# An FNet and GLU kernel: other times and rooms for the tests of its DFT matrices

## The chip, the cores and the metric

The kernel runs on one core of a Trainium2 chip. The metric is the device time of one launch in microseconds, the median of several runs. On the core PE multiplies matrices, DVE and ACT work on vectors, POOL and SP mostly issue transfers here, which 16 DMA engines carry out.

## What is computed

Two layers, each a Fourier mixing step and a gated linear unit, on x of 2048 rows by 640 columns:

```python
def _A_ref(x, dft_seq_re, dft_seq_im, dft_hid_re, dft_hid_im):
    a = jnp.einsum("bsd,ed->bse", x, dft_hid_re)
    b = jnp.einsum("bsd,ed->bse", x, dft_hid_im)
    return jnp.einsum("ts,bse->bte", dft_seq_re, a) - jnp.einsum("ts,bse->bte", dft_seq_im, b)

def _B_ref(x, w_gate, w_up, w_down):
    g = jnp.einsum("bsd,df->bsf", x, w_gate)
    u = jnp.einsum("bsd,df->bsf", x, w_up)
    return jnp.einsum("bsf,fd->bsd", _sigmoid(g) * u, w_down)

x = A_x
for _ in range(2):
    x = x + _A_ref(_layernorm(x, axis=-1), A_dft_seq_re, A_dft_seq_im, A_dft_hid_re, A_dft_hid_im)
    x = x + _B_ref(_layernorm(x, axis=-1), B_w_gate, B_w_up, B_w_down)
```

The matrices are inputs: the sequence matrices are 2048 x 2048, the hidden ones 640 x 640, the weights 640 x 1728 and 1728 x 640.

## The kernel before, in words

The kernel does not multiply by the full DFT matrices. It uses their symmetries (a row and its mirror differ by sign at most) and multiplies folded halves. Since the matrices are inputs, it also tests at run time that the symmetries hold, over the whole of them: it loads a piece and its mirror images, subtracts or adds them on DVE, and sums the squares of what is left on ACT. If at the end the sums are not small, a branch runs `general`, a plain version; with these inputs it does not run.

**The tests.** A test has three parts. `load_rows` (four transfers of 128 KB) and `load_cols` load a piece of the sequence matrices from POOL's queue, `load_hidden_rows` from POOL's and `load_hidden_cols` from SP's a piece of the hidden ones. `test_rows` (L1602, L1603, two of L1605), `test_cols` and the others compare on DVE and put what is left into the list `rest`. `square_rest` takes the oldest entries of `rest` and gives each to `square_sum` (L1579), one ACT instruction over 128 x 768 in most cases, followed by a read of its accumulator. A piece lies in a room, eight units of 128 columns of the buffer `big`. There are two rooms behind the units that the slots use, and test k uses room k % 2, so that a load waits until the square of the test before the last has run.

**The order.** `folded` is run once per layer while the program is built. It fills a list `steps` (what PE does, in order) and a table of jobs: `at(u, f, ...)` puts a job at a due time u, counted in steps. Each step then emits the jobs that are due. A gated step covers two hidden columns (`seven`) and emits its jobs in four portions. Every engine runs its instructions in the order in which they are emitted, and waits for semaphores at the head of its queue. So a due time decides behind what an instruction stands on its engine. A layer has four blocks of 512 rows, each with 14 gated steps (in layer 2 some 11.8 us for two) and 8 steps of `down` (5.6 us each); `block[b]` is the first step of block b.

**Around the tests.** In a gated step PE makes chains of matmuls in PSUM (`products`, L1389). ACT copies an unfinished chain to `big` (`snap`, L1393, 128 x 256) and PE goes on adding to the same bank when the copy is done. DVE adds parts (`part_three`, L1425 and L1426, which frees a bank), ACT takes the sigmoid (L1435), DVE multiplies (`up`, L1445 and L1447), and ACT and DVE split the result into two halves of 16 bits (L1456, L1457). The operands of the next block are made during `down` of the block before: DVE scales rows (`pair_apply`, L598), ACT and DVE split them (`pair_parts`, L616 and L617), and SP transposes them by DMA (`pair_transpose`, L623), in two rounds. Rows of the result leave by an indirect store from POOL's queue (L437). SP loads the weights of the next steps (`load_s`, L1306 to L1312).

**The slots.** All else in `big` comes from `Slots.take` and `give`. The program is built twice: a dry run records at which tick of a clock each slot is taken and given back, `find_homes` then places them, the largest product of size and time first, and prefers a home whose neighbours in time are some ticks away.

The due times of the tests, before:

```python
if first:
    free = (block[1] + 6, block[3] + 13, 42), (d0 - 0.4, d0 + 4.6, 9)
else:
    free = (block[0] + 6, block[0] + 13, 8), (block[1] + 3, block[1] + 14, 10), (block[2] - 6, block[2] + 14, 15)
```

Each triple is a stretch of steps and the number of tests in it; the stretch over the number is the pace.

Of the kernel before, what the change touches and what calls it, by code (L numbers as in the profile page):

```python
# [10 lines left out]
F16 = mybir.dt.float16  # L11
# [5 lines left out]
P = 128  # L17
# [56 lines left out]
WDU = (NF + 1) * 5  # L74
FIX = XU + 2 * XTU + WDU
NEAR = (8, 1)


class Slots:
# [5 lines left out]

    def take(self, n, high):
        k = len(self.asked)
        self.clock += 1
        self.asked.append([n, self.clock, None])
        a = self.homes[k] if self.homes else FIX  # L90
        return Slot(self.big[:, a * UNIT : (a + n) * UNIT], k)

    def give(self, s):
        self.clock += 1
        self.asked[s.k][2] = self.clock


def find_homes(asked):

    area = [n * (t1 - t0) for n, t0, t1 in asked]  # L100
    for near in NEAR:
        first = {}
        for turn in range(40):
            order = sorted(range(len(asked)), key=lambda k: (-first.get(k, 0), -area[k]))
            homes, k = place_in_order(asked, order, near)
            if k is None:
                return homes
            first[k] = first.get(k, 0) + 1
    assert False, f"no room for {asked[k]}"


def place_in_order(asked, order, near):
    homes = [None] * len(asked)
    placed = []
    for k in order:
        n, t0, t1 = asked[k]
# [109 lines left out]
def folded(ctx, tc, pool, dram, big, acc, flag, homes, x, ct, wh, wg, wu, wc, wd, out):  # L226
# [43 lines left out]
            nc.vector.scalar_tensor_tensor(dl, src, s, dh, op0=OP.mult, op1=OP.subtract)  # L270

    def start():
        nc.gpsimd.memset(room(0, 1), 0.0)
# [96 lines left out]

    def junk(n):

        v = room(0, 1).bitcast(F16)
        for _ in range(n):
            nc.tensor.matmul(acc[banks[0]][:, :256], v[:, :P], v, start=True, stop=True)

# [1202 lines left out]
        nc.scalar.activation(v, v, AF.Square, accum_out=new_sum()[:p])  # L1579

    rest = []

    def square_rest(n=1):
        for _ in range(n):
            square_sum(rest.pop(0))

    def room(k, n=CK):
        u = UNITS + CK * (k % 2)
        return big[:, u * UNIT : (u + n) * UNIT]

    def load_rows(r, k):

        v = room(k).rearrange("p (g n c) -> p g n c", g=4, n=2)
        s = 1 + 16 * k
        for g, (row, d) in enumerate(((s, 1), (S - s, -1), (HS - s, -1), (HS + s, 1))):
            nc.gpsimd.dma_start(v[:, g], bass.AP(ct.tensor, (r * S + row) * S, [[P, NS], [d * S, 16], [1, P]]))  # L1596

    def test_rows(r, k):
        v = room(k)
# [3 lines left out]
        nc.vector.tensor_tensor(d, c, d, op=same)  # L1603
        for odd in range(2):
            nc.vector.tensor_tensor(c[:, odd::2], a[:, odd::2], c[:, odd::2], op=other if odd else same)  # L1605
        rest.append(v[:, 2 * P :])

    def load_cols(r, i, k):

        n, row = (P, START[i]) if i < NB else (1, SB)  # L1610
        v = room(k).rearrange("p (g c) -> p g c", g=4)[:n]
        for g, t in ((0, 1 + 256 * k), (2, HS - 256 * (k + 1))):
            nc.gpsimd.dma_start(v[:, g : g + 2], bass.AP(ct.tensor, (r * S + row) * S + t, [[2 * S, n], [HS, 2], [1, 256]]))  # L1613

    def test_cols(r, i, k):
        v = room(k)[: P if i < NB else 1]
# [6 lines left out]
        rest.append(v[:, 256:])  # L1623

    def load_edges(r):

# [24 lines left out]

    def load_hidden_rows(r, k):

        v = room(k)[: 20 * ND].rearrange("p (g n c) -> p g n c", g=2, c=P)
        for g, (row, d) in enumerate(((1 + 80 * k, 1), (D - 1 - 80 * k, -1))):
            nc.gpsimd.dma_start(v[:, g], bass.AP(wh.tensor, (r * D + row) * D, [[P, ND], [d * D, 80], [1, P]]))

    def test_hidden_rows(r, k):
        a, b = (room(k)[: 20 * ND, 4 * P * g : 4 * P * (g + 1)] for g in range(2))
        nc.vector.tensor_tensor(b, a, b, op=OP.subtract if r == 0 else OP.add)  # L1660
        rest.append(b)

    def turns():

# [6 lines left out]

    def load_hidden_cols(r, j):
        n = P if j < 2 else EC - 2 * P
        nc.sync.dma_start(room(3 * r + j)[:n, :D], wh[r, j * P : j * P + n, :])

    def test_hidden_cols(r, j):
        a = room(3 * r + j)[: P if j < 2 else EC - 2 * P, :D]
        b = room(3 * r + j)[: P if j < 2 else EC - 2 * P, D : D + EW - 1]
        nc.vector.scalar_tensor_tensor(b, a[:, : EW - 1], turns()[: b.shape[0]], a[:, EH : EW - 1 : -1], op0=OP.mult,
                                       op1=OP.subtract if r == 0 else OP.add)  # L1680
        rest.append(b)
        nc.vector.tensor_reduce(new_max()[: a.shape[0]], a, axis=AX.X, op=OP.max, apply_absolute_value=True)  # L1682
        nc.vector.tensor_tensor(a[:, 1:EH], a[:, 1:EH], a[:, D - 1 : EH : -1], op=OP.subtract if r == 0 else OP.add)
        rest.append(a[:, 1:EH] if r == 0 else a[:, :EC])
        if r == 1 and j == 0:
            rest.append(a[0:1, EC:])
        if r == 1 and j == 2:
            drop("turns")

# [95 lines left out]
    for layer in range(2):  # L1785
# [158 lines left out]
        if first:  # L1944
            free = (block[1] + 6, block[3] + 13, 42), (d0 - 0.4, d0 + 4.6, 9)
        else:
            free = (block[0] + 6, block[0] + 13, 8), (block[1] + 3, block[1] + 14, 10), (block[2] - 6, block[2] + 14, 15)
        tests = [[(load_rows, test_rows, (r, k)) for k in range(2 * NS)] +
                 [(load_cols, test_cols, (r, i, k)) for i in range(NB + 1) for k in range(2)] for r in range(2)]
        tests = tests[0] + tests[1][:9] if first else tests[1][9:]  # L1950
        for u0, u1, n in free:
            pace = (u1 - u0) / n
            for u in [u0 + pace * k for k in range(n)]:
                load, test, key = tests.pop(0)
                at(u, load, *key)
# [188 lines left out]
```

## Time and profile before

| | before |
|---|---|
| runs, us | 1140.57, 1142.03, 1142.58 (median 1142.03) |
| profiled execution, its own time | 1143.76 us |
| its span in the trace | 1141.9 us |
| granted clock of PE | 0.996 |
| PE busy | 1110.8 us, 97% |
| DVE, ACT, POOL busy | 67%, 47%, 30% |
| bytes moved | 214.72 MB, 188 GB/s on average |

The profile is that of one execution. "Idle before" is how long an engine stood at the head of its queue before an instruction, and the arrow names what ended the wait. The DMA share is the mean busy share of the 16 DMA engines. Line numbers are those of the kernel before; in the changed kernel L598 to L1561 have moved by one.

### The profile page before, as it was taken

To read this page: it belongs to the slowest core of one execution; us is meant where nothing else is said; L and a number is where in the kernel's file an instruction comes from. 1 tells how busy PE (TensorE), PEld (TensorE's weight loads), DVE (VectorE), ACT (ScalarE), POOL (GpSimd) and SP (SyncE) were. 2 spreads that over 40 slices of the span, in tenths; PEclk is the share of its full clock that TensorE was granted. 3 is DMA by queue.
4 is the path that set the end of the run, shared out by engine and by line. 5 is a ranking of instruction groups with operands and counts; after the bars stand their busy time and mean duration, and the time that the engine had idled before them with its cause. 6 is when DMAs were issued, how large, how long until landed. Compare 5 with 4: busy or idle time off the path is not lost. (4 is left out here: it accounts for less than half of the span.)

```text
span 1141.9 us, 23440 instructions
## 1 busy us (share of the span) xinstructions
PE 1110.8 (97%) x9030; PEld 882.3 (77%) x9030; DVE 761.8 (67%) x1678; ACT 537.2 (47%) x1187; POOL 348.1 (30%) x568
## 2 busy tenths in 40 slices
PE   5889999999999999999999999999999999999998
PEld 3668446788878887788878888778877888788875
DVE  7994998856756775486667878834664568526750
ACT  6975583355524653256525545315541455225430
POOL 1001664332546452432350216021453113141000
PEclk9899999999999999999999999999999999999999
DMA  8444685967495767968621665475767864499401
GB/s 250 152 124 151 240 319 157 270 210 244 154 244 182 246 185 152 246 223 291 201 98 57 177 223 160 130 216 179 241 167 174 257 230 150 85 254 284 143 18 38
DMA packets 154447, 214.72 MB, mean 188 GB/s; under 512 B 74655, under 2 KB 99505, under 8 KB 154326
## 3 DMA queue, kind: packets, MB, share of 16 engines
q1 hardware_dynamic: 135622, 165.04, 48.4%
q0 software_dynamic: 18560, 47.93, 14.3%
q8 instruction: 72, 1.18, 0.4%
q14 instruction: 49, 0.40, 0.1%
q10 hardware_dynamic: 144, 0.16, 0.0%
HBM read 173.04 MB, written 25.44 MB: 174 GB/s over the span
## 5 line engine op out<-in xcount | busy, mean ns | idle before, releaser
L1389 PE MATMUL acc<-big 128*128 128x256 f16 x4698 | 517.1, 273 | 4.7 <-ACT big L1393 4.5
L1389 PEld LDWEIGHTS <-big 128*128 128x128 f16 x4698 | 459.6, 98 | 60.1 <-issue 5.7
L1546 PE MATMUL acc<-big 128*128 128x320 f16 x2624 | 357.7, 299 | 0.0
L1546 PEld LDWEIGHTS <-big 128*128 128x128 f16 x2624 | 256.8, 98 | 99.5
L1596 POOL DMA_DIRECT2D big<-in_ct x256 | 174.5, 687 | 270.6 <-DVE big L1605 181.3
L1393 ACT ACTIVATE big<-acc 128x256 f32<-128x256 f32 x348 | 127.7, 380 | 214.7 <-PE acc L1389 212.4
L1579 ACT ACTIVATE big<-big 128x768 f32<-128x768 f32 (+10 forms) x110 | 81.6, 742 | 113.0 <-DVE big L1605 85.5
L1457 DVE TENSOR_TENSOR big<-big 128x512 f16<-128x512 f32 x87 | 59.9, 689 | 105.9 <-ACT big L1456 105.7
L1342 PE MATMUL acc<-big 128*128 128x256 f16 (+1 forms) x705 | 114.6, 325 | 0.5 <-ACT big L672 0.5
L1342 PEld LDWEIGHTS <-big 128*128 128x128 f16 x705 | 68.9, 98 | 45.0 <-issue 0.7
L1435 ACT ACTIVATE big<-big 128x512 f32<-128x512 f32 x87 | 53.3, 627 | 49.1 <-DVE big L1426 48.2
L270 DVE SCALAR_TENSOR_TENSOR big<-big 128x640 f16<-128x640 f32 (+7 forms) x82 | 62.7, 797 | 6.7 <-ACT big L268 6.6
L1561 DVE SCALAR_TENSOR_TENSOR big<-acc,big 128x320 f32<-128x320 f32 x64 | 28.4, 483 | 57.8 <-PE acc L1546 57.8
L1445 DVE SCALAR_TENSOR_TENSOR big<-acc,big 128x256 f32<-128x256 f32 x87 | 36.3, 418 | 41.7 <-PE acc L1389 36.3
L1426 DVE TENSOR_TENSOR big<-big,acc 128x512 f32<-128x512 f32 x87 | 59.2, 681 | 2.0 <-PE acc L1389 1.8
L268 ACT ACTIVATE big<-big 128x640 f16<-128x640 f32 (+7 forms) x82 | 50.9, 657 | 17.3 <-POOL big L1283 6.5
L616 ACT ACTIVATE big<-big 128x384 f16<-128x384 f32 (+2 forms) x48 | 28.8, 648 | 64.1 <-DVE big L598 45.0
L1456 ACT ACTIVATE big<-big 128x512 f16<-128x512 f32 x87 | 54.5, 626 | 9.3 <-DVE big L1447 7.3
L1613 POOL DMA_DIRECT2D big<-in_ct x40 | 27.3, 685 | 96.9 <-ACT big L1393 73.7
L1602 DVE TENSOR_TENSOR big<-big 128x256 f32<-128x256 f32 x64 | 26.7, 416 | 27.4 <-DMA big<-in_ct 26.0
L1603 DVE TENSOR_TENSOR big<-big 128x256 f32<-128x256 f32 x64 | 26.9, 420 | 21.9 <-DMA big<-in_ct 21.9
L979 PE MATMUL acc<-big 128*128 128x256 f16 (+2 forms) x288 | 34.7, 273 | 6.4 <-DVE big L270 2.5
(242 smaller groups left out, 1068.3 us busy)
## 6 DMA issues: line engine op xcount, KB each, us to landing
big<-kept_s SPq DMA_DIRECT2D x84, 512.0 KB, 5.7
big<-kept_w SPq DMA_DIRECT2D x115, 320.0 KB, 5.3
big<-in_ct POOLq DMA_DIRECT2D x256, 128.0 KB, 4.4
big<-kept_w SPq DMA_DIRECT2D x74, 192.0 KB, 6.2
kept_w<-big SPq DMA_DIRECT2D x27, 320.0 KB, 3.7
big<-in_ct POOLq DMA_DIRECT2D x32, 256.0 KB, 4.9
kept_s<-big SPq DMA_DIRECT2D x13, 512.0 KB, 5.7
big<-in_wg SPq DMA_DIRECT2D x18, 320.0 KB, 3.2
```

The costliest lines, as they stand in the source:

```text
L268: nc.scalar.activation(dh, src, AF.Copy, scale=s)
L270: nc.vector.scalar_tensor_tensor(dl, src, s, dh, op0=OP.mult, op1=OP.subtract)
L1342: nc.tensor.matmul(ps, w[wp][:, d * P : (d + 1) * P], xt[:, xp, :], start=(d == 0 and wp == HI and xp == HI), stop=(d == ND - 1 and wp == LO))
L1389: nc.tensor.matmul(ps, wt, xt, start=start and n == 0, stop=n == len(todo) - 1, skip_group_check=not start)
L1393: nc.scalar.activation(dst, ps, AF.Copy)
L1426: nc.vector.tensor_tensor(v, v, other, op=OP.add)
L1435: nc.scalar.activation(v, v, AF.Sigmoid, scale=SG)
L1456: nc.scalar.activation(s.parts[HI], v, AF.Copy)
L1457: nc.vector.tensor_tensor(s.parts[LO], v, s.parts[HI], op=OP.subtract)
L1546: nc.tensor.matmul(held["pd", e][0][:, :EH], held["ht", j].parts[hp][:, i * P : (i + 1) * P], held["w", 2, j].parts[wp][:, e * EH : (e + 1 ...
L1579: nc.scalar.activation(v, v, AF.Square, accum_out=new_sum()[:p])
L1596: nc.gpsimd.dma_start(v[:, g], bass.AP(ct.tensor, (r * S + row) * S, [[P, NS], [d * S, 16], [1, P]]))
```

## The change

Four things are changed, all about the tests.

First, rooms are handed out in turn. `new_room` takes the room that has been free the longest, and a test's last square frees it. Where both are in use, a third is taken from the slots, with `high=LATE`: such a slot does not advance the clock of the dry run, and it is placed after all others, so that it fits into what they leave and moves none of them. Second, due times: in layer 1 the comparison comes at 1.2 of the pace behind the load (1.0 before) and the square at 1.95 (1.7); in layer 2's blocks 1 and 2 at 1.7 (1.4) and 2.6 (1.8). Third, layer 2's first block gets 4 tests (8), the next two 12 and 17 (10 and 15). Fourth, the squares of the hidden rows come at 1.43 of their delay (1.15), the comparisons of the hidden columns 1.6 steps behind the load (1.4) and their squares at 1.45 of that (1.15).

```diff
     def take(self, n, high):
         k = len(self.asked)
-        self.clock += 1
-        self.asked.append([n, self.clock, None])
+        self.clock += high != LATE
+        self.asked.append([n, self.clock, None, high == LATE])
...
-    area = [n * (t1 - t0) for n, t0, t1 in asked]
+    area = [n * (t1 - t0) - 10**9 * late for n, t0, t1, late in asked]
...
     rest = []
+    rooms, n_room, free_rooms = {}, [], [0, 1]
 
     def square_rest(n=1):
         for _ in range(n):
-            square_sum(rest.pop(0))
-
-    def room(k, n=CK):
-        u = UNITS + CK * (k % 2)
-        return big[:, u * UNIT : (u + n) * UNIT]
+            v, done = rest.pop(0)
+            square_sum(v)
+            if done:
+                k = n_room.pop(0)
+                if k > 1:
+                    drop("room", k)
+                else:
+                    free_rooms.append(k)
+
+    def new_room(*key):
+        k = free_rooms.pop(0) if free_rooms else len(rooms)
+        v = take(CK, "room", k, high=LATE).f32 if k > 1 else big[:, (UNITS + CK * k) * UNIT : (UNITS + CK * (k + 1)) * UNIT]
+        rooms[key] = v
+        n_room.append(k)
+        return rooms[key]
...
-            free = (block[0] + 6, block[0] + 13, 8), (block[1] + 3, block[1] + 14, 10), (block[2] - 6, block[2] + 14, 15)
+            free = (block[0] + 6, block[0] + 13, 4), (block[1] + 3, block[1] + 14, 12), (block[2] - 6, block[2] + 14, 17)
...
             pace = (u1 - u0) / n
+            tight = first or u0 < block[1]
...
-                at(u + (1.0 if first else 1.4) * pace, test, *key)
-                at(u + (1.7 if first else 1.8) * pace, square_rest)
+                at(u + (1.2 if first else 1.4 if tight else 1.7) * pace, test, *key)
+                at(u + (1.95 if first else 1.8 if tight else 2.6) * pace, square_rest)
...
-            tests += [(load_hidden_cols, test_hidden_cols, (r, j), 29.8 + 0.9 * (3 * r + j), 1.4) for r in range(2)
+            tests += [(load_hidden_cols, test_hidden_cols, (r, j), 29.8 + 0.9 * (3 * r + j), 1.6) for r in range(2)
...
-                at(block[2] + u + 1.15 * later, square_rest, 1 if load is load_hidden_rows else 3 if key == (1, 0) else 2)
+                at(block[2] + u + (1.43 if load is load_hidden_rows else 1.45) * later, square_rest, 1 if load is load_hidden_rows else 3 if key == (1, 0) else 2)
```

What it does to the order. On ACT, at the start of layer 2's block 2: the last split of the block's operands (L616), squares (L1579), and the first snaps (L1393). Before:

```order
L616 ACTIVATE big<-big 128x768
L1579 ACTIVATE big,dsum<-big 128x768 x3
L1393 ACTIVATE big<-acc_65 128x256
L1393 ACTIVATE big<-acc_438 128x256
L1579 ACTIVATE big,dsum<-big 128x768
L1393 ACTIVATE big<-acc_65 128x256
L1393 ACTIVATE big<-acc_438 128x256
L1393 ACTIVATE big<-acc_437 128x256
L1393 ACTIVATE big<-acc_66 128x256
```

After, one line number further:

```order
L617 ACTIVATE big<-big 128x768
L1580 ACTIVATE big,dsum<-big 128x768 x3
L1394 ACTIVATE big<-acc_65 128x256
L1394 ACTIVATE big<-acc_438 128x256
L1394 ACTIVATE big<-acc_65 128x256
L1394 ACTIVATE big<-acc_438 128x256
L1580 ACTIVATE big,dsum<-big 128x768
L1394 ACTIVATE big<-acc_437 128x256
L1394 ACTIVATE big<-acc_66 128x256
```

The single square has moved from ahead of the second pair of snaps to behind it; it is also another test's, since the squares as a whole come later.

On ACT, in `down` of block 2, where the operands of block 3 are split (L616, four for each of two rounds). Before:

```order
L616 ACTIVATE big<-big 128x384
L616 ACTIVATE big<-big 128x640
L616 ACTIVATE big<-big 128x384
L616 ACTIVATE big<-big 128x768
L1579 ACTIVATE big,dsum<-big 1x768
L616 ACTIVATE big<-big 128x384
L616 ACTIVATE big<-big 128x640
L616 ACTIVATE big<-big 128x384
L616 ACTIVATE big<-big 128x768
L1579 ACTIVATE big,dsum<-big 100x512 x2
```

After:

```order
L617 ACTIVATE big<-big 128x384
L617 ACTIVATE big<-big 128x640
L617 ACTIVATE big<-big 128x384
L1580 ACTIVATE big,dsum<-big 1x768
L617 ACTIVATE big<-big 128x768
L617 ACTIVATE big<-big 128x384
L617 ACTIVATE big<-big 128x640
L617 ACTIVATE big<-big 128x384
L1580 ACTIVATE big,dsum<-big 1x768
L617 ACTIVATE big<-big 128x768
L1580 ACTIVATE big,dsum<-big 100x512 x2
```

The square that stood between the two rounds now stands inside the second, and one that stood ahead of both inside the first.

On POOL, around the two indirect stores of block 1's last rows (L437), with the loads of `load_rows` (L1596). Before:

```order
L1596 DMA big<-in_ct 128x2x128 x12
L437 DMA out<-big,rows 2048x640
L1596 DMA big<-in_ct 128x2x128 x4
L437 DMA out<-big,rows 2048x640
L1596 DMA big<-in_ct 128x2x128 x8
```

After:

```order
L1608 DMA big<-in_ct 128x2x128 x12
L438 DMA out<-big,rows 2048x640
L1608 DMA big<-in_ct 128x2x128 x8
L438 DMA out<-big,rows 2048x640
L1608 DMA big<-in_ct 128x2x128 x12
```

Between the two stores stand the loads of two tests instead of one, and behind them those of three instead of two. PE and SP have the same instructions in the same order as before.

More of the change, by code (lines that the diff above doesn't have):

```diff
@@ L76 @@
 NEAR = (8, 1)
+LATE = 2
 class Slots:
@@ L93, in give @@
     def give(self, s):
-        self.clock += 1
+        self.clock += not self.asked[s.k][3]
         self.asked[s.k][2] = self.clock
 def find_homes(asked):
-    area = [n * (t1 - t0) for n, t0, t1 in asked]
+    area = [n * (t1 - t0) - 10**9 * late for n, t0, t1, late in asked]
     for near in NEAR:
@@ L115, in place_in_order @@
     for k in order:
-        n, t0, t1 = asked[k]
+        n, t0, t1, _ = asked[k]
         ends = {FIX, UNITS - n}
@@ L272, in start @@
     def start():
-        nc.gpsimd.memset(room(0, 1), 0.0)
+        nc.gpsimd.memset(big[:, UNITS * UNIT : (UNITS + 1) * UNIT], 0.0)
         nc.gpsimd.memset(dsum, 0.0)
@@ L371, in junk @@
     def junk(n):
-        v = room(0, 1).bitcast(F16)
+        v = big[:, UNITS * UNIT : (UNITS + 1) * UNIT].bitcast(F16)
         for _ in range(n):
@@ L1581, in folded @@
     rest = []
+    rooms, n_room, free_rooms = {}, [], [0, 1]
     def square_rest(n=1):
         for _ in range(n):
-            square_sum(rest.pop(0))
-    def room(k, n=CK):
-        u = UNITS + CK * (k % 2)
-        return big[:, u * UNIT : (u + n) * UNIT]
+            v, done = rest.pop(0)
[12 more added lines that the diff above has]
+        return rooms[key]
     def load_rows(r, k):
-        v = room(k).rearrange("p (g n c) -> p g n c", g=4, n=2)
+        v = new_room(r, k).rearrange("p (g n c) -> p g n c", g=4, n=2)
         s = 1 + 16 * k
@@ L1598, in test_rows @@
     def test_rows(r, k):
-        v = room(k)
+        v = rooms[r, k]
         a, b, c, d = (v[:, 2 * P * g : 2 * P * (g + 1)] for g in range(4))
@@ L1605, in test_rows @@
             nc.vector.tensor_tensor(c[:, odd::2], a[:, odd::2], c[:, odd::2], op=other if odd else same)
-        rest.append(v[:, 2 * P :])
+        rest.append((v[:, 2 * P :], True))
     def load_cols(r, i, k):
         n, row = (P, START[i]) if i < NB else (1, SB)
-        v = room(k).rearrange("p (g c) -> p g c", g=4)[:n]
+        v = new_room(r, i, k).rearrange("p (g c) -> p g c", g=4)[:n]
         for g, t in ((0, 1 + 256 * k), (2, HS - 256 * (k + 1))):
@@ L1615, in test_cols @@
     def test_cols(r, i, k):
-        v = room(k)[: P if i < NB else 1]
+        v = rooms[r, i, k][: P if i < NB else 1]
         a, d, c, b = (v[:, 256 * g : 256 * (g + 1)] for g in range(4))
@@ L1622, in test_cols @@
         nc.vector.tensor_tensor(c, c, a[:, ::-1], op=other if i in (2, 3) else same)
-        rest.append(v[:, 256:])
+        rest.append((v[:, 256:], True))
     def load_edges(r):
@@ L1652, in load_hidden_rows @@
     def load_hidden_rows(r, k):
-        v = room(k)[: 20 * ND].rearrange("p (g n c) -> p g n c", g=2, c=P)
+        v = new_room("rows", r, k)[: 20 * ND].rearrange("p (g n c) -> p g n c", g=2, c=P)
         for g, (row, d) in enumerate(((1 + 80 * k, 1), (D - 1 - 80 * k, -1))):
@@ L1658, in test_hidden_rows @@
     def test_hidden_rows(r, k):
-        a, b = (room(k)[: 20 * ND, 4 * P * g : 4 * P * (g + 1)] for g in range(2))
+        a, b = (rooms["rows", r, k][: 20 * ND, 4 * P * g : 4 * P * (g + 1)] for g in range(2))
         nc.vector.tensor_tensor(b, a, b, op=OP.subtract if r == 0 else OP.add)
-        rest.append(b)
+        rest.append((b, True))
     def turns():
@@ L1673, in load_hidden_cols @@
         n = P if j < 2 else EC - 2 * P
-        nc.sync.dma_start(room(3 * r + j)[:n, :D], wh[r, j * P : j * P + n, :])
+        nc.sync.dma_start(new_room("cols", r, j)[:n, :D], wh[r, j * P : j * P + n, :])
     def test_hidden_cols(r, j):
-        a = room(3 * r + j)[: P if j < 2 else EC - 2 * P, :D]
-        b = room(3 * r + j)[: P if j < 2 else EC - 2 * P, D : D + EW - 1]
+        a = rooms["cols", r, j][: P if j < 2 else EC - 2 * P, :D]
+        b = rooms["cols", r, j][: P if j < 2 else EC - 2 * P, D : D + EW - 1]
         nc.vector.scalar_tensor_tensor(b, a[:, : EW - 1], turns()[: b.shape[0]], a[:, EH : EW - 1 : -1], op0=OP.mult,
                                        op1=OP.subtract if r == 0 else OP.add)
-        rest.append(b)
+        rest.append((b, False))
         nc.vector.tensor_reduce(new_max()[: a.shape[0]], a, axis=AX.X, op=OP.max, apply_absolute_value=True)
         nc.vector.tensor_tensor(a[:, 1:EH], a[:, 1:EH], a[:, D - 1 : EH : -1], op=OP.subtract if r == 0 else OP.add)
-        rest.append(a[:, 1:EH] if r == 0 else a[:, :EC])
+        rest.append((a[:, 1:EH] if r == 0 else a[:, :EC], (r, j) != (1, 0)))
         if r == 1 and j == 0:
-            rest.append(a[0:1, EC:])
+            rest.append((a[0:1, EC:], True))
         if r == 1 and j == 2:
```

## The prediction

> **What bounds the kernel now.** I read the page first, then PE's waits after the opening, then the timeline around each wait, and last the time ahead of two blocks' starts.
>
> ```profile
> PE 1110.8 (97%) x9030; PEld 882.3 (77%) x9030; DVE 761.8 (67%) x1678; ACT 537.2 (47%) x1187; POOL 348.1 (30%) x568
> L1389 PE MATMUL acc<-big 128*128 128x256 f16 x4698 | 517.1, 273 | 4.7 <-ACT big L1393 4.5
> L1579 ACT ACTIVATE big<-big 128x768 f32<-128x768 f32 (+10 forms) x110 | 81.6, 742 | 113.0 <-DVE big L1605 85.5
> ```
>
> PE is busy for all but 31.1 us of the span of 1141.9, so what the change can win lies in PE's idle time. ACT is at 47%: the squares (L1579) cost nothing by their sum, only by where they stand. PE's waits after the first 100 us (the opening, which the change leaves alone):
>
> ```profile
> PE acc L1389 <- ACT big L1393: 4.5, 6, 1.4
> PE acc L664 <- DVE big L542: 0.6, 1, 0.6
> PE acc L664 <- ACT big L672: 0.2, 1, 0.2
> PE acc L1389 <- DVE big L1426: 0.2, 1, 0.2
> ```
>
> Six waits on snaps (L1393) make 4.5 us of 5.5. The timeline shows why. The same picture three times, at (a) the start of layer 1's block 3, (b) the end of layer 2's block 0, (c) the start of its block 2:
>
> ```profile
> 475.07 0.84 ACT L1579 ACTIVATE big<-big 128x768 f32<-128x768 f32 x1 [3.83 <-DVE big L1605]
> 475.91 0.64 ACT L1393 ACTIVATE big<-acc 128x256 f32<-128x256 f32 x2
> 476.32 0.92 PE L1389 MATMUL acc<-big 128*128 128x256 f16 x7 [0.89 <-ACT big L1393]
> 479.26 0.84 ACT L1579 ACTIVATE big<-big 128x768 f32<-128x768 f32 x1 [2.72 <-DVE big L1605]
> 480.11 1.19 ACT L1393 ACTIVATE big<-acc 128x256 f32<-128x256 f32 x4
> 480.52 1.69 PE L1389 MATMUL acc<-big 128*128 128x256 f16 x14 [1.42 <-ACT big L1393]
> ```
>
> ```profile
> 707.91 0.84 ACT L1579 ACTIVATE big<-big 128x768 f32<-128x768 f32 x1 [3.81 <-DVE big L1605]
> 708.75 0.36 ACT L1393 ACTIVATE big<-acc 128x256 f32<-128x256 f32 x1
> 709.16 1.03 PE L1389 MATMUL acc<-big 128*128 128x256 f16 x8 [0.42 <-ACT big L1393]
> ```
>
> ```profile
> 889.30 1.47 PE L1389 MATMUL acc<-big 128*128 128x256 f16 x12
> 889.64 0.43 DVE L1603 TENSOR_TENSOR big<-big 128x256 f32<-128x256 f32 x1 [1.11 <-DMA big<-in_ct]
> 890.68 0.84 ACT L1579 ACTIVATE big<-big 128x768 f32<-128x768 f32 x1 [4.07 <-DVE big L1605]
> 891.52 1.19 ACT L1393 ACTIVATE big<-acc 128x256 f32<-128x256 f32 x4
> 891.94 1.47 PE L1389 MATMUL acc<-big 128*128 128x256 f16 x12 [1.17 <-ACT big L1393]
> ```
>
> At (c) a test's data land late, DVE compares late, the square waits 4.07 us at the head of ACT's queue and then runs 0.84, and the snaps queued behind it, whose chain PE had finished by 890.77, start at 891.52. At (e), the end of block 3, squares of the hidden columns stand ahead of snaps with no wait:
>
> ```profile
> 1087.12 0.46 ACT L1579 ACTIVATE big<-big 128x321 f32<-128x321 f32 x1
> 1088.03 0.62 ACT L1393 ACTIVATE big<-acc 128x256 f32<-128x256 f32 x2
> 1088.43 2.13 PE L1389 MATMUL acc<-big 128*128 128x256 f16 x18 [0.42 <-ACT big L1393]
> 1089.88 0.47 ACT L1579 ACTIVATE big<-big 128x321 f32<-128x321 f32 x1 [0.39 <-DVE big L1683]
> 1090.35 0.36 ACT L1393 ACTIVATE big<-acc 128x256 f32<-128x256 f32 x1
> 1090.76 0.70 PE L1389 MATMUL acc<-big 128*128 128x256 f16 x5 [0.20 <-ACT big L1393]
> ```
>
> **What one wait costs.** Idle time counts from the modelled end of the last matmul. Twelve matmuls take 1.47 us (889.30) at 0.273 each, so one starts every (1.47 - 0.273) / 11 = 0.109 us. Without the wait the next would have started 0.273 - 0.109 = 0.164 us before the last one's end, so each removed wait gives its idle time plus 0.164. The Trainium skill says the like: by "Perfetto Trace Analysis", section "Identifying the Most-Contended Engine", matmul busy time misleads since matmuls are pipelined, and weight-load time should be taken. Read strictly, with PEld at 77%, PE has room and the removed waits might be worth nothing; the trace speaks against that here, since starts 0.109 us apart are PE's own pace, from row to row. By idle time alone the removed waits would make 3.63 us, by starts 4.45.
>
> **The change, part by part.** PE's and SP's instructions keep their order; squares move on ACT, comparisons on DVE, test loads on POOL in layer 2. No work is added: as many loads, comparisons and squares as before.
>
> Layer 1 (test at 1.2, square at 1.95 of its pace). The square of 475.07 stays ahead of its two snaps, so 0.89 us stays. The square of 479.26 moves behind the first two of the four snaps of 480.11; 1.42 us goes. The snaps behind it are wanted only after PE's next 14 matmuls, which take 1.69 us, and the square runs 0.84: hidden.
>
> Layer 2's first block (4 tests, not 8). The square of 707.91 leaves this place; 0.42 goes. The four tests go to blocks 1 and 2, which hold two more each.
>
> Block 2's start (square at 2.6 paces). The order on ACT shows the two snaps that PE wants at 891.94 directly behind the pair before them; the square that stood between comes four places later. 1.17 goes. Next in line are the first pair's sums on DVE (L1425, L1426), behind which PE continues. The change puts the comparisons of two more tests' data ahead of them. Before, the last of those loads were in by
>
> ```profile
> 892.37 0.42 DVE L1603 TENSOR_TENSOR big<-big 128x256 f32<-128x256 f32 x1
> 893.97 0.41 DVE L1425 TENSOR_TENSOR big<-big 128x256 f32<-128x256 f32 x1
> ```
>
> so a comparison that waits for these same slots of POOL's queue ends near 893.4 (at (c) it takes 1.04 us from the start of L1603, 889.64, to the square that it releases, 890.68), and L1425 could start some 1.3 us ahead of 893.97, at 892.7. It may come 0.7 late, and later by what the loads are late: 0 to 2 us. PE's only wait on L1426 in the program is 0.18 us, so there is little slack known there; I take 0.4.
>
> Block 3's end. The squares of 1086.80 to 1087.58 move behind the snap of 1088.03, those of 1089.07 and 1089.88 several places later: 0.42 + 0.20 go.
>
> Removed: 1.42 + 0.42 + 1.17 + 0.42 + 0.20 = 3.63 us, and with 5 x 0.164 = 0.82, 4.45.
>
> Added: two squares come between the conversions (L616) of blocks 2's and 3's operands, which are then transposed by DMA (L623) for PE's first pair. In block 3:
>
> ```profile
> 979.09 2.31 POOL L1656 DMA_DIRECT2D big<-in_wh  x2 [7.17 <-ACT big L1579]
> 990.10 1.14 DVE L598 TENSOR_SCALAR big<-big,small 128x640 f32<-128x640 f32 x2 [10.93 <-DMA big<-big]
> 991.33 2.51 ACT L616 ACTIVATE big<-big 128x384 f16<-128x384 f32 x4 [12.53 <-DVE big L598]
> 996.77 6.83 SPq L623 DMA_TRANSPOSE big<-big  x2
> big<-big SPq DMA_TRANSPOSE x2, 10.1
> 1010.50 1.69 PE L1389 MATMUL acc<-big 128*128 128x256 f16 x14
> ```
>
> The second transpose is issued half way through 6.83 us, near 1000.2, and lands 10.1 later (the last row, of the stretch from 980 to 1012), near 1010.3; PE starts at 1010.50. There is no margin: lateness goes through to PE. One square lies between the L616s of 991.33: +0.84. That same square now releases the hidden-row load of 979.09, which goes out near 994 instead and so runs beside the second round of transposes, not the first. Its weight, in the stretch 979 to 990:
>
> ```profile
> q0 software_dynamic: 352, 0.42, 23.2%
> ```
>
> That is 0.42 MB and 0.232 x 11 = 2.55 us of all 16 engines. Leaving the first round it lets L598 start up to 2.55 earlier; joining the second it costs up to 2.55. Bounds for the start of block 3: from 2.55 early, which gains nothing as PE is not there yet, to 0.84 + 2.55 = 3.39 late. I take 0.7: the two shares mostly cancel and the square stays. In block 2 a test's loads (0.5 MB, by the same rate 3.0 us) make the same move, with two squares (1.7):
>
> ```profile
> 867.33 5.87 SPq L623 DMA_TRANSPOSE big<-big  x2
> big<-big SPq DMA_TRANSPOSE x2, 9.3
> 884.71 1.47 PE L1389 MATMUL acc<-big 128*128 128x256 f16 x12
> ```
>
> The last one is issued near 870.3 and lands at 879.6, 5.1 us before PE needs it. 4.7 is covered; beyond 5.1 it would count in full.
>
> The third room is placed last, over units that are free meanwhile, and moves no other buffer. I cost it at nothing; a user of the same units that comes up early would wait for a square.
>
> Sum: -4.45 + 0.4 + 0.7 = -3.35.
>
> **The rivals.** (1) *The waits come back under another name.* For it: block 3's start has no margin, DVE carries two more comparisons ahead of L1425, and the square of 475.07 keeps its place while its loads may be issued a little later. Against it: block 2 has 5.1 us, and every test now has more room behind its load. With 2 us at block 3's start and 1.2 more on DVE the sum is -4.45 + 3.2 = -1.25.
>
> (2) *Slower: test loads in the way of block 3's operands.* The engines are full there:
>
> ```profile
> 1000.00:1025.00 25.00, 25.00 (x212) 20.54 (x211) 5.11 (x11) 6.82 (x18) 11.53 (x10) 1.00 1.03 251
> ```
>
> The DMA share (1.03) is the number before the last. If the moved 0.42 MB delays first the transposes (3.39) and then, since nothing is left over, the weights that SP loads behind them (another 2.55), PE loses 5.9, and with 1.2 on DVE 7.1: -4.45 + 7.1 = +2.7. It decides from 4.45 us of lateness in all; below that the change still wins. For it speaks the share of 1.03, against it that the first round is relieved of the same bytes. The Trainium skill has this as a rule ("DMA: Bandwidth & Descriptors", section "Issuing engines are not separate DMA queues"): transfers from SP, ACT and POOL end up on the same 16 engines and interleave, whoever issues them. The trace agrees with it: the transposes' engines are shared at 23.2% by POOL's queue.
>
> (3) *It does not do what it says:* it moves squares, but the ones that hold PE up stay in front of their snaps, as that of 475.07 does. The order on ACT speaks against it for four of the five places. With (c) alone unmoved the sum is -3.35 + 1.33 = -2.0, inside no change.
>
> **How the numbers follow.** The profiled execution took 1143.76 us, 1.73 over the median of 1142.03. -3.35 gives 1140.4, on the median's scale 1138.7, 0.29% faster. A measurement of this kernel can tell about 0.2% from no change: 2.3 us, so faster is below 1139.7 and slower above 1144.3. The forecast (less than -2.3) has 0.53; rival 1 (1140.8) 0.21; rival 3 (1140.0) 0.10; rival 2 (1144.7) 0.16. So faster 0.53, same 0.31, slower 0.16. The low end: all six waits and the DVE one gone, 4.45 + 0.89 + 0.18 + 2 x 0.164 = 5.85, makes 1136.2; that needs a square that did not move, so I take 1136.6. The high end goes to 1144.4, short of rival 2's full price.
>
> **What would show it.** In the changed kernel's trace PE's waits on L1394 (the snap's new line) should fall from 4.5 us in six to about 0.9 in one, at the start of layer 1's block 3; no square should stand in front of the snaps near 891. At block 3's start PE should idle 0 to 1.5 us on a DMA; over 3.4 there is rival 2. A wait of PE on L1427 (the DVE sum) over 1 us in block 2's first pair is rival 1. If the waits on snaps fall as said and the time does not, the step "idle time plus 0.164" is wrong.

## The result and the profile after

The changed kernel takes 1145.09 us (median of 7 runs, 1144.01 to 1147.07), the kernel before 1140.69 (1139.74 to 1142.58) in the same sessions: ratio 1.0036, 95% interval 1.0025 to 1.0048. It is slower by 4.1 us by this ratio and by 4.4 between the medians, where 3.35 faster was forecast, and 1145.09 lies outside the predicted range (1136.6 to 1144.4). The profiled execution of the changed kernel took 1145.01, close to its median.

First the page's line of busy times, then PE's waits after the first 100 us, of the changed kernel (L1390 are the matmuls, L1394 the snaps):

```profile
PE 1111.7 (97%) x9030; PEld 883.4 (77%) x9030; DVE 761.2 (67%) x1678; ACT 538.9 (47%) x1187; POOL 349.1 (31%) x568
PE acc L1390 <- DMA big<-kept_w: 3.2, 1, 3.2
PE acc L1390 <- ACT big L1394: 1.7, 1, 1.7
PE acc L665 <- DVE big L543: 0.6, 1, 0.6
PE acc L665 <- ACT big L673: 0.2, 1, 0.2
```

All six waits on snaps that the prediction listed are gone, also the one it thought would stay. Two new ones stand at the start of layer 2's block 3. The timeline there:

```profile
1014.52 0.69 DVE L1672 TENSOR_TENSOR big<-big 100x512 f32<-100x512 f32 x1 [13.25 <-DMA big<-in_wh]
1015.25 0.63 ACT L1580 ACTIVATE big<-big 100x512 f32<-100x512 f32 x1 [3.48 <-DVE big L1672]
1015.88 1.19 ACT L1394 ACTIVATE big<-acc 128x256 f32<-128x256 f32 x4
1016.29 1.91 PE L1390 MATMUL acc<-big 128*128 128x256 f16 x16 [1.67 <-ACT big L1394]
...
1034.21 4.00 PE L1390 MATMUL acc<-big 128*128 128x256 f16 x23 [3.22 <-DMA big<-kept_w]
```

It is the old picture in a new place: the data of a hidden-row test land late, DVE compares at 1014.52, the square follows, and the snaps queue behind it. Eighteen microseconds later weights are late. At (c), the start of block 2, nothing is left of the old picture; the next square runs in a gap between snaps, and PE does not wait:

```profile
886.86 0.38 ACT L1394 ACTIVATE big<-acc 128x256 f32<-128x256 f32 x1 [0.27 <-PE acc L1390]
887.14 0.84 ACT L1580 ACTIVATE big<-big 128x768 f32<-128x768 f32 x1
887.97 0.65 ACT L1394 ACTIVATE big<-acc 128x256 f32<-128x256 f32 x2
```

Why block 3 is late stands some 40 us further up:

```profile
972.06 0.83 ACT L1580 ACTIVATE big<-big 1x768 f32<-1x768 f32 x1
972.88 0.83 ACT L617 ACTIVATE big<-big 128x768 f16<-128x768 f32 x1
973.27 2.42 POOL L1668 DMA_DIRECT2D big<-in_wh  x2 [14.96 <-ACT big L1580]
973.74 13.52 SPq L624 DMA_TRANSPOSE big<-big  x2
989.32 1.14 DVE L599 TENSOR_SCALAR big<-big,small 128x640 f32<-128x640 f32 x2 [13.07 <-DMA big<-big]
```

The square between the splits releases the first hidden-row load, which goes out at 973.27, together with the first round of transposes. The second scaling (L599) has to wait for that round, until 989.32: 15.6 us after its issue.

### The profile page after: what moved, and what is told of

Its sections match the earlier page's. It is cut to its first block, busy times and chain, and to the rows that moved or that the text cites. A ratio compares the mean times of both kernels' runs of the same rounds, so it can differ in the third digit from the quotient of the medians.

```text
span 1143.2 us, 23440 instructions
## 1 busy us (share of the span) xinstructions
PE 1111.7 (97%) x9030; PEld 883.4 (77%) x9030; DVE 761.2 (67%) x1678; ACT 538.9 (47%) x1187; POOL 349.1 (31%) x568
## 5 line engine op out<-in xcount | busy, mean ns | idle before, releaser
L1390 PE MATMUL acc<-big 128*128 128x256 f16 x4698 | 518.1, 273 | 4.9 <-DMA big<-kept_w 3.2
L1390 PEld LDWEIGHTS <-big 128*128 128x128 f16 x4698 | 460.2, 98 | 60.3 <-DMA big<-kept_w 3.5
L1394 ACT ACTIVATE big<-acc 128x256 f32<-128x256 f32 x348 | 130.7, 383 | 236.2 <-PE acc L1390 232.5
L1427 DVE TENSOR_TENSOR big<-big,acc 128x512 f32<-128x512 f32 x87 | 59.1, 680 | 1.3 <-PE acc L1390 1.1
L1625 POOL DMA_DIRECT2D big<-in_ct x40 | 27.3, 687 | 93.8 <-ACT big L1580 58.2
```

Source lines behind the costliest of these rows:

```text
L1390: nc.tensor.matmul(ps, wt, xt, start=start and n == 0, stop=n == len(todo) - 1, skip_group_check=not start)
L1394: nc.scalar.activation(dst, ps, AF.Copy)
L1427: nc.vector.tensor_tensor(v, v, other, op=OP.add)
```

## The experiments

Every kernel was compared with the kernel before, run beside it. There were three sets.

**Where is the loss, and was the first profile an ordinary one?** The kernel before, profiled again:

> The kernel before, unchanged, profiled once more. Theory A (the loss is new, at the start of layer 2's block 3: PE waits 1.7 us behind a square and 3.2 us for weights there): this profile shows PE's waits on snaps as the first profile did, about 4.5 us in six, and an own time within 1 us of 1142 to 1144. Theory B (the first profile of the kernel before was an unusual execution, and the waits that the change removes are mostly not there in an ordinary one): PE's waits on snaps come to 2.5 us or less, and the own time is near 1140.7.

Measured: 1141.88 us, ratio 1.0002 (0.9992 to 1.0012); the profiled execution took 1140.91.

```profile
PE acc L1389 <- ACT big L1393: 2.2, 5, 0.7
PE acc L664 <- DVE big L542: 0.6, 1, 0.6
PE acc L664 <- ACT big L672: 0.2, 1, 0.2
```

Both numbers are as theory B said, but the waits on snaps are not mostly gone: they come to 2.2 us in five, not 4.5 in six. They differ at two places: at the start of layer 1's block 3, 2.30 us in two in the first profile and 0.36 in one here, and at (c) 1.17 and 0.75. At both a square waits for a comparison of data; at (b) one does too, and there the wait is 0.42 in both profiles.

Layer 1's due times alone, in the kernel before:

```diff
-                at(u + (1.0 if first else 1.4) * pace, test, *key)
-                at(u + (1.7 if first else 1.8) * pace, square_rest)
+                at(u + (1.2 if first else 1.4) * pace, test, *key)
+                at(u + (1.95 if first else 1.8) * pace, square_rest)
```

> The kernel before with only layer 1's due times changed (comparison at 1.2, square at 1.95 of the pace). Theory A: the waits at the start of layer 1's block 3 go, as in the changed kernel's trace (0.89 + 1.42 us and 0.16 for each): 2 to 2.6 us faster than before, ratio near 0.998. Theory B: those waits are rare, so within 0.7 us of before, ratio 0.9995 to 1.0005.

Measured: 1140.19 us, ratio 0.9988 (0.9977 to 0.9999). Its profile has no wait in layer 1's block 3. A gain of 1.4 us, between the two theories.

The changed kernel without this part (1.0 and 1.7 put back):

> The changed kernel with layer 1's due times put back (1.0 and 1.7). Theory A: the loss lies in layer 2 alone, so this is slower than before by as much as the changed kernel or by up to 2.6 us more: +4 to +7 us, ratio 1.0035 to 1.006, with PE waiting 3 us or more for weights in layer 2's block 3. Theory B: the same loss of about +4 us, without the part for layer 1.

Measured: 1145.49 us, ratio 1.0029 (1.0017 to 1.0041). So the loss is in layer 2, if a little smaller than theory A's range, and the wait for weights is 1.3 us, not 3:

```profile
PE acc L1390 <- ACT big L1394: 4.7, 2, 3.5
PE acc L1390 <- DMA big<-kept_w: 1.3, 1, 1.3
PE acc L1390 <- DMA big<-big: 1.0, 1, 1.0
```

The 3.5, the 1.3 and the 1.0 stand in the first 30 us of block 3. Layer 2 is the changed kernel's, yet the lateness divides over square, weights and transposes in another way than in that profile.

The changed kernel with the hidden tests' due times put back (1.6 to 1.4, and 1.43 and 1.45 to 1.15):

> The changed kernel with the hidden matrices' tests put back (squares at 1.15 of their delay, comparisons of the hidden columns 1.4 steps behind the load); three rooms, block counts and the other due times stay changed. Theory A, by the square: the late square in block 3's start goes and a third room is needed less often there, so hidden-row loads no longer crowd the weights: 3 to 5 us faster than the changed kernel, ratio to before 0.9985 to 1.001. Rival C (the two more tests in block 2 and the loads pushed towards block 3 cost it, not the hidden tests' times): no more than 1 us faster than the changed kernel, ratio 1.0025 to 1.004.

Measured: 1145.37 us, ratio 1.0028 (1.0017 to 1.004). These times are not the cause, and the time is as rival C said:

```profile
1014.94 0.69 DVE L1672 TENSOR_TENSOR big<-big 100x512 f32<-100x512 f32 x1 [14.79 <-DMA big<-in_wh]
1015.67 0.63 ACT L1580 ACTIVATE big<-big 100x512 f32<-100x512 f32 x1 [8.41 <-DVE big L1672]
1016.71 1.65 PE L1390 MATMUL acc<-big 128*128 128x256 f16 x7 [5.29 <-ACT big L1394]
```

With both due times the data of this test land near 1014. My theory A, by the hidden tests' own times, fell here. That left the first hidden-row load, and the two squares that stand inside the splits.

**Are two late squares enough?** The kernel before with nothing changed but the due times of the last two sequence squares:

```diff
-                at(u + (1.7 if first else 1.8) * pace, square_rest)
+                tail = not first and u0 > block[1] + 4 and len(tests) < 2
+                at(block[2] + (14.7, 15.88)[1 - len(tests)] if tail else u + (1.7 if first else 1.8) * pace, square_rest)
```

> The kernel before, with nothing changed but the due times of the last two squares of the sequence matrices in layer 2, which put them inside the splits of block 3's operands as the changed kernel has them. Two instructions of ACT move by one and three places. Theory D: this alone costs most of the loss, 3 to 6 us more than before, ratio 1.0025 to 1.005, with PE waiting 3 us or more near the start of block 3. Rival C, and the rival that the third room or the hidden tests' times are to blame: within 1 us of before.

Measured: 1144.9 us, ratio 1.0034 (1.0021 to 1.0048): as slow as the whole change. The same chain as in the changed kernel, first the load and the transposes, then PE:

```profile
971.31 0.83 ACT L1579 ACTIVATE big<-big 1x768 f32<-1x768 f32 x1
972.53 2.43 POOL L1656 DMA_DIRECT2D big<-in_wh  x2 [13.04 <-ACT big L1579]
972.99 13.20 SPq L623 DMA_TRANSPOSE big<-big  x2
988.54 1.14 DVE L598 TENSOR_SCALAR big<-big,small 128x640 f32<-128x640 f32 x2 [13.03 <-DMA big<-big]
...
1014.21 0.69 DVE L1660 TENSOR_TENSOR big<-big 100x512 f32<-100x512 f32 x1 [13.02 <-DMA big<-in_wh]
1015.98 1.25 PE L1389 MATMUL acc<-big 128*128 128x256 f16 x10 [3.07 <-ACT big L1393]
```

The reverse, the changed kernel with only the last two tests at their earlier due times:

```diff
-            tight = first or u0 < block[1]
...
+                tight = first or u0 < block[1] or len(tests) <= 2
```

> The changed kernel, but the last two tests of the sequence matrices in layer 2 keep the earlier due times (1.4 and 1.8 of the pace), so that their squares stand outside the splits of block 3's operands (L617) and free their rooms early. Theory D (the loss comes from these two late squares: they lengthen the splits and hold back the first hidden-row loads by 4 and 14 us, which then run beside both rounds of transposes, and all that follows at block 3's start is late): the first hidden-row load goes out some 3.5 us after block 2's down steps begin, not 11.3, PE's waits near the start of block 3 fall from 4.9 us to under 1, and the time is 4 to 6 us below the changed kernel's, ratio to before 0.997 to 0.9995. Rival C (two more tests in block 2, more bytes there): no change, ratio 1.002 to 1.004.

Measured: 1139.45 us, ratio 0.9985 (0.9974 to 0.9996): its median is 5.6 us below the changed kernel's, which rules out rival C. But the expectation of under 1 us of waits failed: in its profile PE waits 3.4 us for transposes and 1.7 for weights. Its runs spread from 1137.96 to 1143.09, and the profiled one (1142.77) is among the longest. The second hidden-row load, at 974.1, now went out beside the first round instead.

Two rooms of their own for the first two hidden-row loads, with the squares left inside the splits:

```diff
-        k = free_rooms.pop(0) if free_rooms else len(rooms)
+        fresh = key in (("rows", 0, 0), ("rows", 0, 1))
+        k = free_rooms.pop(0) if free_rooms and not fresh else len(rooms)
```

> The changed kernel, but the first two hidden-row loads take a room of their own from the slots, so that they need not wait for the late squares, which stay inside the splits. Theory D1 (the held-back loads are the cause): the loads go out at 3.5 and about 13 us after the down steps begin, the waits at block 3's start fall below 1.5 us, 3 to 5 us faster than the changed kernel, ratio 0.9985 to 1.0005. Theory D2 (the squares inside the splits are the cause: 1.6 us more in the chain from split to transpose): the transposes start as late as in the changed kernel, and less than 1.5 us is won, ratio 1.002 to 1.0035.

Measured: 1137.72 us, ratio 0.9968 (0.9956 to 0.998), and no wait is left at block 3. That is more than theory D1 allowed, and the loads went out 0.6 and 20.3 us after the down steps began, not 3.5 and 13. But this doesn't separate D1 from D2: the extra rooms did not fit behind the other slots, so the placement started over and 195 of 819 slots got other addresses, among them those that make the second scaling wait for the first transposes.

The hidden rows' squares later still (1.43 to 1.9):

> The changed kernel with the hidden rows' squares later still (1.9 of their delay, not 1.43), so that they stand behind more snaps. If the square ahead of the snaps is what holds PE at block 3's start, the wait on snaps there (1.7 us in the changed kernel's trace) goes and 1 to 4 us are won, ratio 1.000 to 1.003. Theory D (the data are late, so PE meets the next late thing, the weights): under 1 us won, ratio 1.003 to 1.0045, with the wait for weights 3 us or more.

Measured: 1141.31 us, ratio 1.0003 (0.9993 to 1.0013). The square's wait is gone and 2.1 us for weights stay, as D said of the next late thing, but 3.8 us are won, more than it allowed. It is confounded too: 208 slots moved.

**The load or the squares?** The changed kernel without the first two hidden-row tests, all addresses as in the changed kernel:

```diff
             for load, test, key, u, later in tests:
+                if load is load_hidden_rows and key in ((0, 0), (0, 1)):
+                    continue
```

> The changed kernel without the first two of the eight hidden-row tests (their loads, comparisons and squares are left out, so part of the tests is not made); the late squares stay inside the splits, and every buffer has the address that it has in the changed kernel. Theory D1 (a hidden-row load beside the first round of transposes makes that round twice as long, and this is what makes block 3's start late): the second scaling (L599) starts about 17 us after block 2's down steps begin, not 27, PE's waits at block 3's start fall below 1 us, 4 to 7 us faster than the changed kernel, ratio to before 0.995 to 0.999. Theory D2 (the squares inside the splits): the scaling starts at 25 or later and at most 2 us are won.

Measured: 1138.05 us, ratio 0.9968 (0.9956 to 0.998), with no wait of PE at block 3. Both squares are still inside the splits:

```profile
970.73 0.83 ACT L1580 ACTIVATE big<-big 1x768 f32<-1x768 f32 x1
972.41 5.63 SPq L624 DMA_TRANSPOSE big<-big  x2
980.15 1.14 DVE L599 TENSOR_SCALAR big<-big,small 128x640 f32<-128x640 f32 x2 [5.24 <-DMA big<-big]
982.85 0.83 ACT L1580 ACTIVATE big<-big 1x768 f32<-1x768 f32 x1
```

The first round takes 7.7 us instead of 15.6. So the squares inside the splits cost little by themselves, and the loss needs the loads that they hold back, as D1 says. Both loads are gone here, so this run does not say which of them counts. The same step in the kernel before, without its second hidden-row test (`key == (0, 1)`):

> The kernel before without the second hidden-row test (its load, comparison and square are left out). Its load is the one that runs beside the first round of transposes there. Theory D1: that round takes about 7 us instead of 14, the second scaling (L598) starts about 17 us after the down steps begin, not 24, and the second round ends some 7 us ahead of PE; the time changes little (0 to -1 us), since PE did not wait there before. If the load does not matter, the scaling stays at 24.

Measured: 1141.63 us, ratio 1.0 (0.9991 to 1.0009); the round takes 8.3 us, and nothing is won, as expected: the kernel before bears the load beside its transposes without a wait, but with nothing to spare.

Only four addresses, in the kernel before:

```diff
+    homes = find_homes(asked)
+    for f0, b0, f1, b1 in ((648, 655, 656, 657), (733, 740, 741, 742)):
+        homes[f1], homes[b1] = homes[f0], homes[b0]
+    return homes
```

> The kernel before with four addresses changed: in layer 2's blocks 2 and 3 the second pair's scaled rows take the units of the first pair's scaled rows, not those of the first pair's halves, which the first round of transposes reads; the second pair's halves take those of the first pair's halves. Rival P (the addresses, which also changed in the run with rooms of their own and in that with still later squares, are what helps): the second scaling (L598) starts within 2 us of the first round's issue, not 14 later, and the operands are ready 1 to 2 us earlier; alone in this kernel worth 0 to -1 us, since PE did not wait there. Theory D1: the splits (L616) then wait for the first round instead, and the second transposes are issued no more than 2 us earlier; 0 within 0.1%.

Measured: 1140.38 us, ratio 0.9991 (0.998 to 1.0001). That cannot be told from nothing. But its trace shows the sign of rival P: the second scaling starts 3.0 us after the first round's issue, not 14, and the second round goes out 25.3 us after the down steps begin, not 30.8 (second profile of the kernel before). That is 5.5 us earlier, where D1 allowed 2. So the other addresses in the two runs above may have made part of their gain, and how much stays open.

Last, a version without the collision and with all tests: the last two sequence tests early as above, and the second hidden-row load behind the indirect store on POOL's queue, where it goes out near 991, when the first round is long over:

```diff
             for load, test, key, u, later in tests:
+                if load is load_hidden_rows and key == (0, 1):
+                    u = 18.6
```

> The kernel with the last two sequence tests at their earlier due times (as in the run of that name), and the second hidden-row load moved behind the indirect store on POOL's queue, so that no test's load runs beside the first round of transposes; all addresses as in the changed kernel. Theory D1: the waits for transposes (3.4 us there) and for weights (1.7 us) go, PE's idle time after the opening falls to 1 to 2 us, 1138 us, ratio 0.996 to 0.998, as low as with the two rooms of their own. If the other addresses were what helped in that run, no gain: 0.998 to 0.9995.

Measured: 1137.95 us (1137.78 to 1138.59), ratio 0.9967 (0.9954 to 0.998). The round takes 8.8 us, and PE's idle time after the opening is 0.9 us, none of it from tests. It computes all that the kernel before and the changed kernel do and is faster than both, at the changed kernel's addresses. The second load goes out nearly as late here (29.8 us after the down steps begin) as in the changed kernel (31.2), though behind the store and not ahead of it, and nothing is lost. That speaks for the load beside the first round as the one that counts.

```profile
965.29 2.42 POOL L1668 DMA_DIRECT2D big<-in_wh  x2 [7.73 <-ACT big L1580]
971.43 6.68 SPq L624 DMA_TRANSPOSE big<-big  x2
980.26 1.13 DVE L599 TENSOR_SCALAR big<-big,small 128x640 f32<-128x640 f32 x2 [5.76 <-DMA big<-big]
```

## Why the prediction was wrong, point by point

**What bounds the kernel, and the waits removed: right.** PE's waits on snaps behind squares went, all six. The last kernel, which loses nothing at block 3, is 3.6 us faster than before, and the forecast said 3.35. That the two are so close is luck: the waits removed were worth less than forecast (below), and the +0.4 and +0.7 us that were set against them are not in this kernel.

**Idle time plus 0.164 us: right.** PE's instructions stand in the same order in all kernels, so the start of each can be subtracted between two traces. Between the second profile of the kernel before and that without two tests, the lag grows by 0.52 us at the wait of 0.364 us in layer 1, and by 0.91 at that of 0.748 at (c).

**The size of the waits: too large.** 4.45 us was read from one execution that ran long (1143.76 beside a median of 1140.69). In the second profile five waits of 2.2 us idle cost 2.2 + 5 x 0.164 = 3.0. That alone would have left a gain, not a loss.

**Block 3's start: the step that failed.** The prediction took +0.7 us, between 0 and 3.39. Subtracting starts, the changed kernel is 0.75 us behind the last kernel from the opening to 1009, and 7.48 from 1038 to the end: it loses 6.7 us there and nothing elsewhere. With these two sizes the sum is -3.0 + 6.7 = +3.7 us, near the measured 4.1. Three things were wrong in the step.

First, the load that "leaves the first round". The one of the trace (the second hidden-row load) did leave it, and went out at 993.23. But the first, which had gone out before the round, took its place: its room, too, is freed by a square that now stands inside the splits. I followed one load past the transposes and not the one ahead of it in the same queue.

Second, its price. I took the load's own share of the engines, 2.55 us. The transposes' share tells another story, in the stretch of the first round, of the changed kernel and then of that without two tests:

```profile
q1 hardware_dynamic: 4416, 1.11, 88.1%
q0 software_dynamic: 352, 0.42, 16.0%
...
q1 hardware_dynamic: 4416, 1.11, 88.3%
```

The last row has no load beside it. The same 4416 packets and 1.11 MB take 88.1% of 16.2 us (973.2 to 989.4) beside the load, 14.3 us of all engines, and 88.3% of 7.8 us (972.4 to 980.2) alone, 6.9. The load makes the transposes' packets twice as slow: 7.4 us, three times what I priced. A load that starts 3 us into the round, as in the kernel before, does nearly as much:

```profile
973.41 6.95 SPq L623 DMA_TRANSPOSE big<-big  x2
976.41 2.31 POOL L1656 DMA_DIRECT2D big<-in_wh  x2 [7.17 <-ACT big L1579]
987.41 1.14 DVE L598 TENSOR_SCALAR big<-big,small 128x640 f32<-128x640 f32 x2 [10.92 <-DMA big<-big]
```

That is 14.0 us (second profile), so the change makes the round 1.6 us longer. Counted from the start of block 2's down steps, the second scaling starts at 24.1 us there (963.3) and at 27.3 in the changed kernel (962.0). The other 1.6 us lie ahead of the round: the square in the first split, and a comparison that now stands ahead of the first scaling on DVE. Neither was in the sum. Together the second round goes out 3.2 us later.

Third, what is late next. I looked at the transposes' landing, and that was nearly in time: PE does not wait for it in the changed kernel's profile. Counted from the down steps, the last transpose lands at 44.7 us, in the second profile of the kernel before at 44.1. What stands behind the second round is later:

```profile
995.54 0.34 SPq L443 DMA_DIRECT2D out<-big  x1
1001.51 1.10 POOL L438 DMA_INDIRECT out<-big,rows  x1 [5.97 <-DVE big L1672]
1002.62 2.38 POOL L1668 DMA_DIRECT2D big<-in_wh  x2
...
1020.13 0.74 SPq L1307 DMA_DIRECT2D big<-kept_w  x1
```

The third hidden-row load (1002.62) stands on POOL's queue behind a store of result rows (1001.51). The arrow names a comparison on DVE, but what the store waits for is most likely SP's store of other rows (995.54), which lands at 1000.68: in six traces (this one, the second profile of the kernel before, and four of the experiments) POOL's store starts 0.8 to 0.9 us after the landing of SP's, whatever DVE does then. SP's store goes out 3.2 us later than before and lands after 5.1 us, not 2.8. So the third load goes out 5.6 us later (40.6 and 35.1), and then follow its comparison, its square, and the snaps behind it. That is the mechanism that the change removes elsewhere.

The weights are loaded behind the second round on SP's queue, and the first of them go out 4.9 us later (41.5 and 36.7). The load whose end PE awaits at 1034.21 is that of 1020.13: it took 14.0 us to land, the same load before (1018.24) took 7.9. No run separates the part of the third load from that of the weights' own place in the queue. Rival 2 had the cause (test loads in the way of block 3's operands, then the weights) with +2.7 us and a chance of 0.16; the trace's zero margin, which I had quoted, deserved more.

**The 0.4 us on DVE in block 2: not seen.** PE has no wait on L1427.

## What to carry to other kernels

When a job is put later so that it doesn't block a queue, ask what it releases: here a square freed a room, the room a load, and the load fell on a round of transposes with no slack behind it. Follow every load that waits for the moved instruction, also those that were harmless where they stood. And take a second profile before pricing waits that depend on when data land: here they came to half.

## What the runs showed of the hardware

A transfer's cost to its neighbour is not its own share. Packets of a DMA transpose took about 25 ns alone and 52 beside a 0.42 MB load of 352 packets from POOL's queue (6.9 and 14.3 us of 16 engines over 4416 packets).

A long wait of PE can cost more than its idle time. The windows around the wait of 3.22 us in the changed kernel (length, PE busy, PEld, DVE, ACT, POOL, granted clock, DMA share, GB/s):

```profile
1031.00:1034.20 3.20, 0.00 (x0) 0.00 (x0) 1.85 (x4) 0.38 (x1) 0.61 (x1) 0.89 1.04 260
1034.20:1035.00 0.80, 0.79 (x4) 0.57 (x5) 0.00 (x0) 0.00 (x0) 0.00 (x0) 0.50 1.10 251
1035.00:1036.00 1.00, 1.00 (x7) 0.69 (x5) 0.00 (x0) 0.29 (x2) 0.00 (x0) 0.50 1.02 226
1036.00:1037.00 1.00, 1.00 (x7) 0.68 (x6) 0.00 (x0) 1.00 (x3) 0.00 (x0) 0.53 1.04 247
1037.00:1038.00 1.00, 1.00 (x11) 0.90 (x10) 0.00 (x0) 0.73 (x3) 0.00 (x0) 1.00 1.07 233
```

For 2.8 us PE runs at half speed: 0.8 x 0.50 + 1.00 x 0.50 + 1.00 x 0.47 = 1.4 us more. With 1.67 + 3.22 of idle time and two times 0.164 that makes 6.6 of the 6.7 us lost at block 3. The wait of 1.67 us had no such effect; that of 3.07 us in the kernel with two late squares had it, from 1.1 us after PE went on. The Trainium skill, "TensorE: Matmul & The Clock Gate", section "What's actually happening", gives half speed after at least one idle window of about 3.4 us; here 3.07 us were enough.

But length alone does not decide. The changed kernel with its last two tests early has a wait of 3.40 us, and the clock stays full in it and behind it:

```profile
1005.77:1009.16 3.39, 0.00 (x0) 0.00 (x0) 0.00 (x0) 0.00 (x0) 1.37 (x2) 1.00 0.97 186
1009.16:1013.00 3.84, 3.84 (x36) 3.44 (x36) 1.46 (x3) 0.77 (x2) 3.84 (x4) 1.00 1.04 356
```

In these traces the granted clock changes only at whole multiples of 3.41 us from its first change (the full clock before the drop at 1033.53 had lasted 972.8 us, 285 times 3.413). Laid on this grid, the waits after the opening sort themselves. The clock fell at the end of each stretch of 3.41 us in which PE had idled 2.15 us or more (2.15, 2.29, 2.52 and 2.54 in four kernels), and not where it had idled 1.93 or less. The wait of 3.40 us fell on two stretches, with 1.6 and 1.8 in each. This is read from a few waits, and no run was made to test it.
